# Converting w_out two feature blocks at a time, and two small sums as fp32r products, in a fused attention / soft-MoE / feed-forward kernel

## The chip, the cores and the metric

One core of one Trainium2 chip runs the whole program. The metric is device microseconds of one execution, from the start of the program to the last output in memory. The kernel before takes 477.78 us, the median of three executions (477.72 to 479.6).

## What is computed

Three stages run one after the other; the change lies in the third.

```python
x = _attn_ref(q, k, v, mem_k, mem_v)          # chunked attention, 4 x 768 tokens, 8 heads of 64
x = _moe_ref(x, phi, w1, w2)                  # soft mixture: c @ slot_out, c is 3072 x 32, slot_out 32 x 512
h = x @ w_in                                  # w_in 512 x 2048
r = np.maximum(h, 0.0)
g = s * (r * r) + b
out = g @ w_out                               # w_out 2048 x 512, out 3072 x 512
```

Since x = c @ slot_out, the kernel forms m = slot_out @ w_in (32 x 2048) once and h = c @ m. The constant b goes through w_out as b times its column sums, which are added to the output at the end, so the products only see r * r.

## The kernel before

**Two 16-bit halves.** TensorE multiplies fp32r operands at one rate and plain f32 operands as two instructions of a slower one. The large products are done in fp32r, and each operand is split into a high part (a cast to fp32r) and a low part (value minus high part): `ghi`/`glo` for r * r, `w_hi`/`w_lo` for w_out. Three products of a pair (high x high, low x high, high x low) make one output. w_in and w_out come in as 16-bit halves of their words, and every block has to be put together on ScalarE and VectorE before it is split.

**One block of w_out, 128 rows x 512.** `stage_a(k)` is a ScalarE copy with a scale (`cv_act`, line 579). `stage_d(k, 0..5)` are six VectorE instructions: a shift (589), an or with the sign (591), a mask (593), the low half times the exponent (600), value minus `w_hi` (791), plus the low half (793), which writes `w_lo`. `stage_w(k)` is the cast to `w_hi` on ScalarE (798). The table `cq` says at which step k a block is converted: w_out blocks 0 to 7 at steps 0, 2, .. 14, four quarters each of w_in's column groups 2 and 3 at steps 16 to 30, w_out blocks 8 to 15 at steps 32 to 46. Two buffers `cvs` alternate.

**The item loop.** `items` holds 128 pairs (run, f): a run is 384 tokens and a stretch of w_out's 16 blocks. The first 16 items are blocks 0 to 7 of token groups 0 and 1 in turn, the next 32 all blocks of groups 2 and 3 in turn, then groups 4 to 7 alone, then blocks 8 to 15 of groups 0 and 1. Step n emits `emit_h(n)` (line 825, one product of 384 columns into a PSUM tile of the tag "s", which has two buffers), the nine products of 512 columns of older items (`emit_o`, line 877, of item n-3, six of them; `emit_o2`, line 889, of item n-4, three), `emit_relu`, `emit_sq`, `emit_ghi` (ScalarE, 831, 835, 839: relu out of PSUM, square, cast) and `emit_g` (VectorE, 842: the low part of item n-1). When a run ends, its three PSUM tiles are copied out (894 and 896), and the next run on the same tiles waits for that. Steps 0 to 3 are written out by hand ahead of the loop: the ramp.

**Order.** The schedule is manual: each engine runs its instructions in the order in which the program emits them.

**m.** Column group 0 of m (blocks 0 to 3 of w_in's 2048 columns) is done in the ramp by `m_part` and `m_split`. Group fb = 1, 2, 3 comes at step n of `M_AT = (4, 26, 34)`: `emit_m` (806) puts four partial sums on four groups of 32 partitions of a PSUM tile of tag "s", a ScalarE copy (808) brings them to `mps`, and at step n+1 `emit_m2` (812) adds them with a 0/1 matrix `stks_all` in a plain f32 product of 512 columns, into another tile of tag "s"; `m_split` (817 on ScalarE, 818 on VectorE) writes the high and the low part into `mpack`, the stationary operand of line 825. In each step `emit_m` and `emit_m2` stand behind `emit_relu`, `emit_sq` and `emit_ghi`.

**Column sums.** From step 48 to 63 `wsum_add` adds `w_hi` and `w_lo` of all blocks on VectorE, and at step 64 `colsum` (852) sums over partitions by an f32 product with ones; line 853 scales it into `bias`.

**Loads.** `load_w` issues one weight load on the sync engine's queue, in a fixed order. Behind the first ones the loads go round a ring of three areas, each issued as soon as the last use of the block it overwrites (`last_use`) has been emitted.

Of the kernel before, what the change touches and what calls it, by code (L numbers as in the profile page):

```python
# [8 lines left out]
F32 = mybir.dt.float32  # L9
F32R = mybir.dt.float32r  # L10
I32 = mybir.dt.int32
# [24 lines left out]
def kernel(  # L36
# [81 lines left out]
    with tc.manual_schedule():  # L118
# [60 lines left out]
        raw_of = {("i", fb, j): ("wi", 2 * fb + j // 2) for fb in range(1, NFB) for j in range(4)}  # L179
        raw_of.update({("o", f): ("wo", f // 2) for f in range(NF)})  # L180
        last_use = {}
        for k, key in sorted(cq.items()):
            if raw_of[key] not in last_use:
                order.append(raw_of[key])
            last_use[raw_of[key]] = k
# [5 lines left out]
        def load_w(n, cap=None):  # L191
            for _ in range(n):
                i = wnext[0]
                if i < (len(order) if cap is None else cap):
                    src = srcs[order[i][0]][order[i][1]]
                    p = at_[order[i]] if i < npre else (16 + (i - npre) % NRG) * SLOT
# [369 lines left out]
        soT4 = area(15 * SLOT + 1536, KD, 4, NS)  # L566
        sos_r = Ring(14 * SLOT + 1536, 2, 256)
# [150 lines left out]
        for i in range(16):  # L718
            emit_w2(i)
            if i == 4:  # L720
                left.close()
                pk_p = ctx.enter_context(tc.tile_pool(name="pk", bufs=1, reuse_waits="tile"))
                cpack = pk_p.tile([128, NT], F32R, name="cpack")
                mpack = pk_p.tile([128, 128 * NF], F32R, name="mpack")
            if i in (3, 7, 11):
# [28 lines left out]
        w_hi, w_lo = tiles("whi", NF, DM, F32R), tiles("wlo", NF, DM, F32R)  # L754
        os_g, mps = tiles("os", 3, DM), tiles("mps", 1, DM)[0]
        r_g, r2_g = (tiles(x, 2, UT) for x in ("r", "r2"))
        ghi_g, glo_g = tiles("ghi", LA + 2, UT, F32R), tiles("glo", LA + 2, UT, F32R)
        wsum, bias = tiles("wsum", 1, DM)[0], tiles("bias", 1, DM)[0]
        ones = tiles("ones", 1, 128)[0]
        nc.gpsimd.memset(ones, 1.0)  # L760
# [11 lines left out]

        def stage_a(k):
            key = cq.get(k)
            if key:
                if key[0] == "i":
                    w = wi_src(key[1], key[2])
                else:
                    w = wt[raw_of[key]].rearrange("p (f d t) -> p f d t", f=2, t=2)[:, key[1] % 2]
# [20 lines left out]
        def emit_m(fb):  # L800
# [129 lines left out]
        stage_a(0)  # L930
# [3 lines left out]
        stages(0, 0)  # L934
# [5 lines left out]
        stages(0, 1)  # L940
# [23 lines left out]
        stage_a(4)  # L964
        stages(2, 2, 3)
        emit_g(3)
        stages(2, 4, 5)
        stages(4, 0)
        for n in range(LA + 1, len(items) + LA + 1):
# [29 lines left out]
            stage_d(n + 1, 0)  # L999
            if 48 <= n < 64:  # L1000
# [80 lines left out]
```

## Time and profile before

| | |
|---|---|
| median of 3 executions | 477.78 us (477.72 to 479.6) |
| the profiled execution, whole | 481.1 us |
| its span, first to last instruction | 479.3 us |
| TensorE matmul busy | 455.8 us (95%), 3960 instructions |
| VectorE busy | 309.6 us (65%) |
| ScalarE busy | 307.6 us (64%) |
| GpSimd busy | 84.1 us (18%) |
| mean granted TensorE clock | 0.999 of 2.4 GHz |

The 1.8 us between 479.3 and 481.1 lie around the span. Busy shares are means over stages: attention until about 124 us, the expert products (bound by the loads of their weights) until about 171 us, the ramp of the last stage until about 190 us, and then the item loop until 474 us. A busy TensorE says little by itself, since matmuls overlap and a waiting one can be counted as busy. What ends the execution is read from the chain of waits, and what a step costs from the starts of line 825, which comes once in each step.

### The profile page before, as it was taken

The page shows a single profiled execution, that of the slowest core. Times are in us where ns is not written, and L with a number is a line of the kernel's source. Part 1 is how long each engine was busy: PE and PEld are TensorE (multiplying, and loading weights), DVE is VectorE, ACT ScalarE, POOL GpSimd, SP SyncE. Part 2 cuts the span into 40 slices and gives each one's busy share as a digit, 9 for nine tenths or more (in the row PEclk, how much of TensorE's full clock was granted, in tenths as well). Part 3 has the DMA queues.
Part 4 walks back from the last instruction along what each step waited for, and adds up shares of the span by engine and source line. Part 5 has one row for each costly group of instructions (what it writes and reads, how often), then busy time and mean ns, then how long its engine had stood idle before and what let it go on. Part 6 is the DMA issues. An engine that isn't in the chain of part 4 may idle for free.

```text
span 479.3 us, 10204 instructions
## 1 busy us (share of the span) xinstructions
PE 455.8 (95%) x3960; PEld 342.8 (72%) x3960; DVE 309.6 (65%) x685; ACT 307.6 (64%) x635; POOL 84.1 (18%) x154
## 2 busy tenths in 40 slices
PE   6889998999999878999999999999999999999996
PEld 5656666665545365886787888887888888888885
DVE  5768888886485867999485999985624224223232
ACT  4556665665134357998686888666666666666660
POOL 6665655560000000000000000006700000000000
PEclk9999999999999999999999999999999999999999
DMA  8999999999999932333332000003101001001011
GB/s 302 371 406 403 399 408 401 392 384 402 384 408 383 416 137 88 116 150 96 115 142 88 1 1 0 1 0 131 69 0 67 0 1 66 0 1 65 2 66 66
DMA packets 20576, 83.04 MB, mean 173 GB/s; under 512 B 2736, under 2 KB 2864, under 8 KB 14640
## 3 DMA queue, kind: packets, MB, share of 16 engines
q1 hardware_dynamic: 20528, 82.39, 44.5%
q8 instruction: 31, 0.51, 0.4%
q14 instruction: 17, 0.14, 0.1%
HBM read 76.09 MB, written 6.29 MB: 172 GB/s over the span
## 4 chain that ended last, share of the span: by engine, by line
PE 68%; DVE 12%; DMA 10%; ACT 4%; issue 2%; POOL 2%; SPq 1%; DVEq 0%; POOLq 0%; ACTq 0%
PE g L877 11%; PE lp L877 5%; PE pt L877 5%; PE x L877 5%; PE g L889 5%; PE xt L877 5%; PE s L825 4%; DMA keys<-in_w_out_dram 4%; DMA vals<-in_vm_dram 3%; PE s L630 3%; PE x L325 3%; PE lp L889 3%; PE pt L889 3%; PE xt L889 3%; PE x L889 3%; PE s L285 2%
## 5 line engine op out<-in xcount | busy, mean ns | idle before, releaser
L842 DVE TENSOR_TENSOR glo<-r,ghi 128x384 fp32r<-128x384 f32 x128 | 76.3, 600 | 81.4 <-ACT ghi L839 81.2
L831 ACT ACTIVATE r<-s 128x384 f32<-128x384 f32 x128 | 62.7, 490 | 52.7 <-PE s L825 52.4
L835 ACT ACTIVATE r<-r 128x384 f32<-128x384 f32 x128 | 67.2, 525 | 9.7 <-DVE glo L842 5.6
L839 ACT CAST ghi<-r 128x384 fp32r<-128x384 f32 x128 | 65.4, 511 | 3.4
L825 PE MATMUL s<-cpack,mpack 128*128 128x384 f32 x128 | 44.7, 352 | 1.9 <-DVE mpack L818 1.9
L301 ACT ACTIVATE seg<-seg 128x384 f32<-128x384 f32 x32 | 28.7, 897 | 19.2 <-DVE seg L312 15.3
L889 PE MATMUL g<-wlo,ghi 128*128 128x512 f32 x128 | 40.2, 394 | 0.0
L877 PE MATMUL g<-whi,ghi 128*128 128x512 f32 x126 | 39.7, 394 | 0.3 <-DVE mpack L818 0.3
L877 PE MATMUL g<-whi,glo 128*128 128x512 f32 x126 | 39.4, 393 | 0.0
L864 POOL TENSOR_TENSOR keys<-keys,bias 128x512 f32<-128x512 f32 x6 | 8.4, 1430 | 169.4 <-DVE bias L853 169.4
L263 POOL TENSOR_SCALAR keys<-keys 64x416 f32<-64x416 f32 x63 | 33.6, 533 | 14.2 <-DMA keys<-in_kq_dram 7.4
L285 PE MATMUL s<-keys 128*32 128x128 f32 x768 | 30.3, 291 | 5.0 <-POOL keys L267 4.2
L325 PE MATMUL x<-vals,seg 128*32 128x128 f32 x744 | 28.0, 275 | 3.6 <-DMA vals<-in_vm_dram 2.9
L825 PEld LDWEIGHTS s<-cpack,mpack 128*128 128x128 f32 x128 | 23.9, 188 | 9.5 <-DVE mpack L818 2.0
L325 PEld LDWEIGHTS x<-vals,seg 128*32 128x32 f32 x744 | 20.5, 109 | 13.3 <-DVE seg L309 4.6
L889 PEld LDWEIGHTS g<-wlo,ghi 128*128 128x128 f32 x128 | 24.0, 188 | 5.2
L877 PEld LDWEIGHTS g<-whi,glo 128*128 128x128 f32 x126 | 23.7, 188 | 5.4
L285 PEld LDWEIGHTS s<-keys 128*32 128x32 f32 x768 | 19.5, 113 | 11.0 <-POOL keys L267 6.5
L319 ACT COPY seg<-pt 128x384 f32<-128x384 f32 x32 | 15.2, 476 | 18.5 <-PE pt L317 17.6
L877 PEld LDWEIGHTS g<-whi,ghi 128*128 128x128 f32 x126 | 23.7, 188 | 4.4 <-DVE mpack L818 0.7
L877 PE MATMUL lp<-whi,ghi 128*128 128x512 f32 x63 | 25.5, 404 | 0.9 <-DVE vals L896 0.9
L877 PE MATMUL pt<-whi,glo 128*128 128x512 f32 x64 | 25.3, 395 | 0.7 <-DVE glo L842 0.7
(255 smaller groups left out, 990.6 us busy)
## 6 DMA issues: line engine op xcount, KB each, us to landing
seg<-in_w_dram SPq DMA_DIRECT2D x27, 1024.0 KB, 8.5
keys<-in_kq_dram SPq DMA_DIRECT2D x32, 396.0 KB, 7.3
vals<-in_vm_dram SPq DMA_DIRECT2D x64, 192.0 KB, 6.6
keys<-in_w_in_dram SPq DMA_DIRECT2D x5, 1024.0 KB, 5.1
keys<-in_w_out_dram SPq DMA_DIRECT2D x5, 1024.0 KB, 4.9
out_dram<-os SPq DMA_DIRECT2D x18, 256.0 KB, 2.1
vals<-in_w_in_dram SPq DMA_DIRECT2D x3, 1024.0 KB, 7.7
vals<-in_w_out_dram SPq DMA_DIRECT2D x3, 1024.0 KB, 4.8
```

What stands on the lines that cost most here:

```text
L263: (nc.vector if h and u == 0 else nc.gpsimd).tensor_scalar(out=stream(kz[rows, h], 0, CH), in0=k[rows, UT * h:UT * h + (NCU + 1) * CH].rea ...
L285: nc.tensor.matmul(out=o, lhsT=qt[:, 32 * c:32 * c + 32], rhs=kz[:, :, at:at + WIN], start=True, stop=not (first or last))
L301: nc.scalar.activation(out=p_r[u], in_=sm_r[u].rearrange("p t h (a r) -> p t r (h a)", a=2), func=AF.Exp, scale=scale)
L319: nc.scalar.copy(out=pts_r[u], in_=pt)
L325: nc.tensor.matmul(out=xp[32 * r:32 * r + 32, t], lhsT=pts_r[u][:, 32 * c:32 * c + 32], rhs=vbuf[u // 2 % 2][:, u % 2, :, 64 * c:64 * c + ...
L825: nc.tensor.matmul(out=hq, lhsT=mpack[:, 128 * f:128 * f + 128], rhs=cpack[:, b * UT:(b + 1) * UT], start=True, stop=True)
L831: nc.scalar.activation(out=r_g[n % 2], in_=h_t.pop(n), func=AF.Relu)
L835: nc.scalar.activation(out=r2_g[n % 2], in_=r_g[n % 2], func=AF.Square)
L839: nc.scalar.copy(out=ghi_g[n % (LA + 2)], in_=r2_g[n % 2])
L842: nc.vector.tensor_tensor(out=glo_g[n % (LA + 2)], in0=r2_g[n % 2], in1=ghi_g[n % (LA + 2)].bitcast(F32), op=ALU.subtract)
L877: nc.tensor.matmul(out=o_t[r_][t], lhsT=gt[:, 128 * t:128 * t + 128], rhs=w_hi[f], start=(f == r_[1] and gt is ghi), stop=False)
L889: nc.tensor.matmul(out=o, lhsT=ghi[:, 128 * t:128 * t + 128], rhs=w_lo[f], start=False, stop=(f == f1 - 1))
```

## The change

It touches only the last stage and its preparations.

- Blocks 0 and 1 of w_out are converted as before at steps 0 and 2. Blocks 2 to 15 are converted in seven pairs (`pair_a`, `pair_d` 0 to 3, `pair_hi`) with instructions of 2 x 512 columns, the pair i beginning at step `PS[i]` (4, 7, 10, 31, 34, 38, 42); `pair_a` comes one step earlier, `pair_hi` one step later.
- `stage_a(0)` moves behind the first `m_split`, and the first VectorE steps of block 0 behind the second.
- `mps` is split in two: `mph` (ScalarE cast) and `mpl` (VectorE, value minus `mph`), and `emit_m2` becomes two fp32r products that accumulate. `colsum` does the same with `wsum`.
- In the item loop, `emit_m` and `emit_m2` move ahead of `emit_relu`, `emit_sq`, `stage_a` and `emit_ghi` of their step.
- Two constants, the 0/1 matrix and ones, are cast to fp32r on ScalarE during the expert products; the GpSimd memset of `ones` goes.
- `bias` shares its memory with `wsum`. The ring of loads lies in other areas, `soT4` and `sos_r` move, and the second of the first three ring loads is issued one product group later (the loop over 16 products: at 10, 11 and 14 in place of 10, 10 and 14).

```diff
         for j in range(8):
+            cq[16 + 2 * j] = ("i", 2 + j // 4, j % 4)
+        for j in range(2):
             cq[2 * j] = ("o", j)
-            cq[16 + 2 * j] = ("i", 2 + j // 4, j % 4)
-            cq[32 + 2 * j] = ("o", 8 + j)
...
+        PS = {1: 4, 2: 7, 3: 10, 4: 31, 5: 34, 6: 38, 7: 42}
+        last_use = {("wi", 4 + j // 2): 16 + 2 * j for j in range(8)}
+        last_use.update({("wo", i): n + 1 for i, n in PS.items()})
+        last_use["wo", 0] = 2
+        RAW = [17 * SLOT, 18 * SLOT, 14 * SLOT]
...
+                nc.scalar.copy(out=stkr, in_=stks_all)
+                nc.scalar.activation(out=onesr, in_=stks_all, func=AF.Copy, scale=0.0, bias=1.0)
...
-            if i == 10:
-                load_w(2)
-            if i == 14:
+            if i in (10, 11, 14):
                 load_w(1)
...
+        def pair_a(i):
+            nc.scalar.activation(out=pair[:, :, 0, :], in_=pair_w(i)[:, :, :, 1].bitcast(F32), func=AF.Copy,
+                                 scale=2.0 ** -112)
+        def pair_hi(i):
+            nc.scalar.copy(out=two(wh_all, i), in_=pair[:, :, 2, :])
+        def pair_d(i, step):
+            h, lf, a = (pair[:, :, j, :] for j in range(3))
+            hi, ai, w = h.bitcast(I32), a.bitcast(I32), pair_w(i)
+            if step == 0:
+                nc.vector.tensor_scalar(out=hi, in0=hi, scalar1=3, scalar2=None, op0=ALU.logical_shift_left)
+                nc.vector.scalar_tensor_tensor(out=ai, in0=w[:, :, :, 1], scalar=SIGN, in1=hi, op0=ALU.bitwise_and,
+                                               op1=ALU.bitwise_or)
+            elif step == 1:
+                nc.vector.tensor_scalar(out=hi, in0=ai, scalar1=EXPM, scalar2=None, op0=ALU.bitwise_and)
+                nc.vector.scalar_tensor_tensor(out=lf, in0=w[:, :, :, 0].bitcast(U32), scalar=2.0 ** -52, in1=h,
+                                               op0=ALU.mult, op1=ALU.mult)
+            elif step == 2:
+                nc.vector.tensor_tensor(out=a, in0=a, in1=two(wh_all, i).bitcast(F32), op=ALU.subtract)
+            else:
+                nc.vector.tensor_tensor(out=two(wl_all, i), in0=a, in1=lf, op=ALU.add)
...
-            nc.scalar.copy(out=mps, in_=mp)
+            halves(mp)
+
+        def halves(x):
+            nc.scalar.copy(out=mph, in_=x)
+            nc.vector.tensor_tensor(out=mpl, in0=x, in1=mph.bitcast(F32), op=ALU.subtract)
+
+        def sum_of(out, lhsT):
+            for x in (mph, mpl):
+                nc.tensor.matmul(out=out, lhsT=lhsT, rhs=x, start=(x is mph), stop=(x is mpl))
...
-            nc.tensor.matmul(out=mr, lhsT=stks_all, rhs=mps, start=True, stop=True)
+            sum_of(mr, stkr)
...
-            nc.tensor.matmul(out=c, lhsT=ones, rhs=wsum, start=True, stop=True)
+            halves(wsum)
+            sum_of(c, onesr)
...
-        stage_a(0)
         m_part(mpa, (2, 3), ha)
         m_split(mpa, 0, ha)
         m_part(mpb, (2, 3), hb)
-        stages(0, 0)
+        stage_a(0)
         m_split(mpb, 0, hb)
...
-        stage_a(4)
         stages(2, 2, 3)
+        pair_a(1)
         emit_g(3)
         stages(2, 4, 5)
-        stages(4, 0)
...
+            if n in M_AT:
+                emit_m(M_AT.index(n) + 1)
+            if n - 1 in M_AT:
+                emit_m2(M_AT.index(n - 1) + 1)
             emit_relu(n)
             emit_sq(n)
             stage_a(n + 1)
             emit_ghi(n)
-            if n in M_AT:
-                emit_m(M_AT.index(n) + 1)
-            if n - 1 in M_AT:
-                emit_m2(M_AT.index(n - 1) + 1)
...
+            for i, p0 in PS.items():
+                if n == p0 + 1:
+                    pair_hi(i)
+                if 0 <= n - p0 < 4:
+                    pair_d(i, n - p0)
+                if n == p0 - 1:
+                    pair_a(i)
```

## Rows read from the trace of the kernel before

**Rows 1.** Windows: each engine's busy us (instructions), clock, DMA share, GB/s
```profile
151.70:171.00 19.30, 16.06 (x186) 8.75 (x182) 12.08 (x22) 6.81 (x17) 0.20 (x1) 1.00 1.01 416
...
215.00:220.00 5.00, 4.14 (x17) 2.60 (x16) 4.90 (x9) 4.71 (x10) 0.00 (x0) 1.00 0.02 2
...
260.00:300.00 40.00, 40.00 (x179) 33.01 (x178) 38.63 (x70) 33.29 (x68) 0.00 (x0) 1.00 0.00 1
```

**Rows 2.** Timeline of PE, line 825, at the first runs' end: start us, us, instruction
```profile
212.82 0.34 PE L825 MATMUL s<-cpack,mpack 128*128 128x384 f32 x1
...
215.08 0.34 PE L825 MATMUL s<-cpack,mpack 128*128 128x384 f32 x1
...
217.79 0.34 PE L825 MATMUL s<-cpack,mpack 128*128 128x384 f32 x1
...
221.36 0.34 PE L825 MATMUL s<-cpack,mpack 128*128 128x384 f32 x1
```

**Rows 3.** Timeline of the ramp's head, in brackets the idle time before and its releaser
```profile
170.74 0.66 ACT L579 ACTIVATE seg<-keys 128x512 f32<-128x512 f32 x1 [2.38 <-DMA keys<-in_w_out_dram]
171.31 0.25 ACT L817 CAST mpack<-pt 128x128 fp32r<-128x128 f32 x1
...
171.94 0.62 PE L825 MATMUL s<-cpack,mpack 128*128 128x384 f32 x2 [1.85 <-DVE mpack L818]
...
174.30 0.39 PE L877 MATMUL pt<-whi,ghi 128*128 128x512 f32 x1
```

**Rows 4.** Timeline of PE later in the ramp: the two longest waits
```profile
183.72 1.13 PE L812 MATMUL s<-mps,stk 128*128 128x512 f32 x2 [0.82 <-ACT mps L808]
...
188.50 0.50 PE L877 MATMUL pt<-whi,glo 128*128 128x512 f32 x1 [0.70 <-DVE glo L842]
```

**Rows 5.** Chain of waits, 196 to 205 us: start us, us, engine, tile, line
```profile
198.61 0.42 DVE keys L589
199.03 0.47 DVE glo L842
...
203.00 0.42 DVE seg L589
```

**Rows 6.** Timeline of DVE in the same stretch: start us, us, instruction
```profile
202.39 0.69 DVE L793 TENSOR_TENSOR wlo<-keys 128x512 fp32r<-128x512 f32 x1
...
203.34 0.55 DVE L842 TENSOR_TENSOR glo<-r,ghi 128x384 fp32r<-128x384 f32 x1
```

**Rows 7.** Instructions of line 817 by form: duration ns min/median/max, first and last start
```profile
L817 ACT CAST mpack<-s x3: 583/586/586, 186.6 to 259.9; 128x512 fp32r<-128x512 f32 x3
...
L817 ACT CAST mpack<-g x1: 366/366/366, 175.4 to 175.4; 128x256 fp32r<-128x256 f32 x1
```

**Rows 8.** Groups by line and form, 195 to 480 us: busy us, mean ns, idle before
```profile
L579 ACT ACTIVATE keys<-keys 128x512 f32<-128x512 f32 x6 | 4.0, 659 | 0.0
```

**Rows 9.** Chain of waits around the second group of m: start us, us
```profile
235.05 1.21 PE s L806 x12
236.26 0.37 PE s L825
...
238.70 0.86 PE s L812 x2
239.96 0.47 PE g L877 x2
```

**Rows 10.** Chain of waits at step 64
```profile
325.37 0.86 PE s L852 x2
```

**Rows 11.** Waits, 166 to 222 us: us in total, times, longest
```profile
PEld s L806 <- ACT r L831: 0.4, 1, 0.4
```

**Rows 12.** Timeline of ACT in steps 26 and 27, idle time before in brackets
```profile
233.01 0.49 ACT L831 ACTIVATE r<-s 128x384 f32<-128x384 f32 x1 [0.25 <-PE s L825]
...
236.31 0.59 ACT L808 COPY mps<-s 128x512 f32<-128x512 f32 x1 [1.70 <-PE s L806]
236.79 0.50 ACT L831 ACTIVATE r<-s 128x384 f32<-128x384 f32 x1
```

More of the change, by code (lines that the diff above doesn't have):

```diff
@@ L175 @@
         for j in range(8):
+            cq[16 + 2 * j] = ("i", 2 + j // 4, j % 4)
+        for j in range(2):
             cq[2 * j] = ("o", j)
-            cq[16 + 2 * j] = ("i", 2 + j // 4, j % 4)
-            cq[32 + 2 * j] = ("o", 8 + j)
[L179 to L185, printed above, removed]
+        PS = {1: 4, 2: 7, 3: 10, 4: 31, 5: 34, 6: 38, 7: 42}
+        last_use = {("wi", 4 + j // 2): 16 + 2 * j for j in range(8)}
+        last_use.update({("wo", i): n + 1 for i, n in PS.items()})
+        last_use["wo", 0] = 2
+        order += [("wo", i) for i in range(4)] + [("wi", i) for i in range(4, 8)] + [("wo", i) for i in range(4, 8)]
+        RAW = [17 * SLOT, 18 * SLOT, 14 * SLOT]
         srcs = {"w1": w1, "w2": w2, "wi": w_in, "wo": w_out}
@@ L195, in load_w @@
                     src = srcs[order[i][0]][order[i][1]]
-                    p = at_[order[i]] if i < npre else (16 + (i - npre) % NRG) * SLOT
+                    p = at_[order[i]] if i < npre else RAW[(i - npre) % NRG]
                     if p is SPLIT:
@@ L565 @@
         cvs = [area((14 + i) * SLOT, 3, 512) for i in range(2)]
-        soT4 = area(15 * SLOT + 1536, KD, 4, NS)
-        sos_r = Ring(14 * SLOT + 1536, 2, 256)
+        soT4 = area(16 * SLOT + 1024, KD, 4, NS)
+        sos_r = Ring(16 * SLOT + 1536, 2, 256)
         ck_r = [area(p, 4, 4, NS).bitcast(F32R) for p in range(11 * SLOT, 11 * SLOT + NT, 512)]
@@ L724 @@
                 mpack = pk_p.tile([128, 128 * NF], F32R, name="mpack")
+                stkr = pk_p.tile([128, 128], F32R, name="stkr")
+                onesr = pk_p.tile([128, 128], F32R, name="onesr")
+                nc.scalar.copy(out=stkr, in_=stks_all)
+                nc.scalar.activation(out=onesr, in_=stks_all, func=AF.Copy, scale=0.0, bias=1.0)
             if i in (3, 7, 11):
@@ L752, in tiles @@
             return [g_p.tile([128, w], dt, name=f"{name}{i}") for i in range(n)]
-        w_hi, w_lo = tiles("whi", NF, DM, F32R), tiles("wlo", NF, DM, F32R)
-        os_g, mps = tiles("os", 3, DM), tiles("mps", 1, DM)[0]
+        wh_all, wl_all = (tiles(x, 1, NF * DM, F32R)[0] for x in ("whi", "wlo"))
+        w_hi, w_lo = ([t[:, DM * f:DM * f + DM] for f in range(NF)] for t in (wh_all, wl_all))
+        os_g, (mph, mpl) = tiles("os", 3, DM), tiles("mp", 2, DM, F32R)
         r_g, r2_g = (tiles(x, 2, UT) for x in ("r", "r2"))
         ghi_g, glo_g = tiles("ghi", LA + 2, UT, F32R), tiles("glo", LA + 2, UT, F32R)
-        wsum, bias = tiles("wsum", 1, DM)[0], tiles("bias", 1, DM)[0]
-        ones = tiles("ones", 1, 128)[0]
-        nc.gpsimd.memset(ones, 1.0)
+        wsum = tiles("wsum", 1, DM)[0]
+        bias = wsum
         HF = NF // 2
@@ L771, with pair_w, two @@
         h_t, o_t = {}, {}
+        cvs[:] = [area(15 * SLOT + 1536 * x, 3, 512) for x in range(2)]
+        pair = area(15 * SLOT, 3072).rearrange("p (x j f) -> p x j f", x=2, j=3)
+        def pair_w(i):
+            return wt["wo", i].rearrange("p (f d t) -> p f d t", f=2, t=2)
+        def pair_a(i):
[3 more added lines that the diff above has]
+            nc.scalar.copy(out=two(wh_all, i), in_=pair[:, :, 2, :])
+        def two(t, i):
+            return t[:, 2 * DM * i:2 * DM * (i + 1)].rearrange("p (x f) -> p x f", x=2)
+        def pair_d(i, step):
[13 more added lines that the diff above has]
+                nc.vector.tensor_tensor(out=two(wl_all, i), in0=a, in1=lf, op=ALU.add)
         def stage_a(k):
@@ L778, in stage_a @@
                 else:
-                    w = wt[raw_of[key]].rearrange("p (f d t) -> p f d t", f=2, t=2)[:, key[1] % 2]
+                    w = wt["wo", key[1] // 2].rearrange("p (f d t) -> p f d t", f=2, t=2)[:, key[1] % 2]
                 cv_act(key, k // 2 % 2, w)
@@ L939 @@
         m_part(mpc, range(KD), hc)
-        stages(0, 1)
+        stages(0, 0, 1)
         nc.vector.tensor_copy(out=w_hi[0], in_=cv[cq[0]][2])
```

## The prediction, made before the changed kernel ran

> **What bounds the kernel now.** I read the windows first, then the starts of line 825, then the chain of waits, and the timelines of ScalarE and VectorE only where the chain leaves TensorE. The windows [rows 1] show three regimes: up to 171 us the queues move 416 GB/s and the weights set the pace; from 215 to 220 us VectorE is busy for 4.90 of 5 us while TensorE has a hole (4.14); from 260 to 300 us TensorE is busy throughout, though VectorE nearly is as well (38.63 of 40). The starts of line 825 tell what each step costs: 2.26 us when nothing waits (212.82 to 215.08), but 2.71 and 3.57 us for the two steps at the end of the first runs, 0.45 + 1.31 = 1.76 us too much [rows 2]. From 221.36 us to the last product at about 474 us the chain of waits stays on TensorE. So what TensorE loses or saves there moves the end one for one, and work taken from ScalarE and VectorE there is worth nothing. Before 221 us there are four places to gain: 1.85 us ahead of h(0) [rows 3], 0.82 us ahead of the sum of m's group 1 and 0.70 us ahead of item 4's low product [rows 4], and the 1.76 us.
>
> **The head of the ramp.** ScalarE waits 2.38 us for the first block of w_out, and the first copy of m stands behind that conversion; h(0) starts at 171.94 us [rows 3]. Turned round, h(0) leaves the path. Late next is `w_hi[0]`: the conversion still starts at 170.74 and takes until 171.3, the second copy of m and its VectorE part stand ahead of the shift (about 0.6 us together), and shift, or and cast take some 1.6 us, so about 173.5 us. Item 0's first product ran at 174.30 [rows 3]: -0.8 us.
>
> **Pairs.** Converting one block costs VectorE 203.00 - 198.61 = 4.39 us less two low parts of 0.47, so 3.45 us in six instructions [rows 5]. From 384 to 512 columns an instruction grows from 0.55 to 0.69 us [rows 6], 1.1 ns a column; that leaves about 0.1 us an instruction that does not grow, 0.6 us for six. A pair thus takes 6.3 us instead of 6.9 (an estimate from these rows; 6.9 if nothing is saved). VectorE before needs 4.39 us for two steps of 4.52: no reserve. After, three pairs save 1.8 us and the last ends at step 13 rather than 15, so VectorE is ahead when the first runs end, and the 1.76 us of [rows 2] go: -1.76. If a backlog is left, some or all of that comes back. At ScalarE an instruction grows by 0.86 ns a column (586 against 366 ns for 256 more [rows 7]); the conversion becomes 1.10 us instead of twice 0.66 [rows 8], the cast about the same, some 0.4 us less per pair, which nobody on the path feels.
> But a pair is ready later: item 4 needs `w_hi[2]` after a shift, an or and a cast that are each up to twice as long, some 1.2 us more in all, and `w_lo` follows likewise. I put the waits for the two at 1.0 and 0.6 us where 0.70 us stood [rows 4], and 0.1 us more at item 1: +1.0. Bounds: -0.7 if the pair is early, +2 if both wait an instruction longer. The later pairs begin three or four steps ahead of use, and their loads are issued eight or more steps ahead: nothing, as long as VectorE, which with 6.3 + 3 x 0.47 = 7.7 us needs 0.9 us more than three steps of 2.26, makes that up in the steps without a pair.
>
> **The two-part sums.** An f32 sum of 512 columns took 0.86 us, two fp32r products take 2 x 0.235 = 0.47 [rows 9], so -0.4 us at each of four places. In the ramp (step 4) the copy no longer stands behind relu, square and cast; but `pair_a(1)`, 1.1 us long, now does stand ahead of it, the low part (about 0.7 us on VectorE) must be there as well, and relu(4) behind the copy holds h(5). I take these as equal to the 0.82 us of before [rows 4], so -0.4 net, with 0.8 us to either side. At step 64 the copy of `wsum` starts when ScalarE is through with the step's cast, and the low part follows, 0.6 + 0.7 us, of which the products of the step cover about half; the second product waits some 0.5 us, so that the step costs 0.1 to 0.4 us more than with the 0.86 us [rows 10]; I take +0.2. The bias, which replaces `wsum` in place, waits for nothing new.
>
> **Copies ahead of relu, steps 26, 27, 34 and 35.** Here is the cost. Tag "s" has two buffers. In order they go to h(26), m's partial sums, h(27), the sum, h(28): h(27) needs the one that relu(26) reads, h(28) the one that relu(27) reads. That such a wait is real shows in the ramp, where line 806 waits 0.4 us for relu [rows 11]. Before, relu(26) ran at 233.01 us, while TensorE did the step's products, and the copy waited until 236.31 with nothing urgent behind it [rows 12]. Now relu(26), its square and its cast queue behind the copy: copy at 236.31, relu at 236.79, over at 237.29, and only then h(27), which ran at 236.26 [rows 9]. That is 1.05 us, of which 0.1 to 0.2 us was lost there already (0.37 us for a product of 0.18). The same a step later: from the end of the sum 0.03 + 0.48 us until relu, 0.50 us of relu, then h(28): again 1.0 to 1.2 us, less the 0.40 us that the sum saves. One group: +1.6 us by these rows, +2.0 if the array gives its results as late behind the shorter products (a lone product lasts 0.39 us [rows 3] in a slot of 0.235, 0.16 us twice). Two groups: +3.2 to +4.0, I take +3.6. On VectorE's queue glo(25) and the conversions wait behind the low part and behind `m_split`'s; they have slack, since item n's low part is read at step n+3.
> The row shows ScalarE holding back a copy whose input was ready, for a load that the copy did not need [rows 3]. The Trainium skill (TensorE: Matmul & The Clock Gate, Architectural detail) says that ScalarE and VectorE are strictly first in, first out, and that TensorE alone pulls weight loads ahead. By that rule, with which the trace agrees, the sum keeps its +3.6 us; an engine that let relu pass would give the time of the first rival.
>
> **Moved and small.** The two casts of constants (128 columns, about 0.25 us each) and the new areas of the ring lie in the expert products, where loads at 416 GB/s set the pace [rows 1]; the ring's second load, issued later on the sync engine's queue, still stands behind several us of queued bytes. If that cover were gone, it would come a few us later, but it is needed some 8 us after the first. GpSimd's memset held nobody on the path.
>
> **Sum.** -0.8 - 1.76 + 1.0 - 0.4 + 3.6 + 0.2 = +1.8 us. The profiled execution took 481.1 us in all, so 482.9 on its own terms. It is 3.3 us longer than the median; were some of that the first block of w_out landing later than it usually does, h(0) would usually not wait for it and up to 0.8 us of gain would be lost. On the median: 477.8 + 1.8 = 479.6 us. Its own range, by the bounds above, is 477.8 to 481.6.
>
> **Rivals.**
> *Faster: relu does not hold TensorE.* If h(27) and h(28) found a free buffer, the two groups would give 2 x -0.4 instead of +3.6: 479.6 - 4.4 = 475.2. For it: the sums are 0.4 us cheaper each. Against it: [rows 11], and all eight PSUM tiles (two "s", two "g", "pt", "x", "xt", "lp") being in use.
> *Slower: the pair's strided parts wait for each other as one area.* The parts of `pair` interleave in memory; if waits are set for the whole range, the mask waits for the cast to `w_hi` (about 1.1 us) and the next pair's conversion for the subtraction. VectorE's 7.7 us for three steps become 8.8 against 6.78, 2.0 us late at each of the three gaps of three steps; of these 6.0 us some 1.5 are caught up: +4.5, so 484.1. It decides as soon as a pair's chain passes three steps and the reserve behind it. Against it: nothing before has such a wait.
> *The run's end stays.* If VectorE is still late at step 18, the 1.76 us remain: 481.4.
>
> **How the numbers follow.** Forecast 0.62, faster rival 0.14, waits within the pair 0.12, run's end 0.12. About 0.5%, 2.4 us, is what a measurement of this kernel can tell from no change: 475.4 to 480.2. Three fifths of the forecast lie inside it, the rest above; of the faster rival two thirds lie below. So faster 0.10, same 0.43, slower 0.47. Range: the forecast's own and the run's end, stretched down to the faster rival: 475.0 to 482.0, which leaves out the waits within the pair and the tails.
>
> **What would show it.** Line 825 of steps 27, 28, 35 and 36 should start about 1 us late behind a wait for line 831, with relu right behind the copy on ScalarE; the two products of a sum should stand 0.23 us apart; the steps at the first runs' end should take 2.26 us with no wait for an evacuation; item 0's first product should come about 0.8 us earlier; and there should be a short TensorE wait for the low part ahead of the column sums. I am wrong if TensorE waits for nothing at those four steps, or if a pair's instructions wait for each other across engines.

## The result, and the profile after

The changed kernel takes 481.8 us, the median of nine executions (480.64 to 484.09), beside 478.74 us for the kernel before on the same chip (nine executions, 477.72 to 480.36). The ratio is 1.0073, with a 95% interval of 1.005 to 1.0095: slower by 2.4 to 4.5 us. The forecast was +1.8 us. Its sign and its main mechanism hold, but the size is short by about half.

The waits of TensorE in the last stage of the kernel after, in us in total, times and longest (line 873 is relu, 867 h, 920 and 932 the products of the items, 786 the pair's cast to `w_hi`, 805 its `w_lo`, 846 the low part of a sum, 850 the sum):

```profile
PE s L867 <- ACT r L873: 4.6, 5, 1.1
PE pt L920 <- ACT whi L786: 0.9, 1, 0.9
PE s L850 <- DVE mp L846: 0.5, 2, 0.3
PE pt L932 <- DVE wlo L805: 0.5, 1, 0.5
```

The first line is the one the prediction asked for: h waits for relu, about 1.07 us at each of four steps and once, for 0.35 us, in the ramp. No wait for an evacuation is left. The starts of h at the first runs' end, where [rows 2] had 2.71 and 3.57 us, are 2.26 us apart:

```profile
211.43 0.34 PE L867 MATMUL s<-cpack,mpack 128*128 128x384 f32 x1
213.69 0.34 PE L867 MATMUL s<-cpack,mpack 128*128 128x384 f32 x1
215.95 0.34 PE L867 MATMUL s<-cpack,mpack 128*128 128x384 f32 x1
218.20 0.34 PE L867 MATMUL s<-cpack,mpack 128*128 128x384 f32 x1
```

Two windows answer to [rows 1] (busy us and instructions of TensorE, weight loads, VectorE, ScalarE, GpSimd; clock, DMA share, GB/s):

```profile
213.00:218.00 5.00, 5.00 (x24) 4.12 (x23) 4.93 (x10) 4.76 (x10) 0.00 (x0) 1.00 0.23 39
264.00:304.00 40.00, 40.00 (x179) 33.04 (x178) 33.51 (x48) 32.25 (x61) 0.00 (x0) 1.00 0.00 1
```

At the run ends TensorE has no hole any more. VectorE is as busy as before in this one window, but over the whole steps from h(18) to h(21) it has less to do. Here are these steps in the kernel before, then in the kernel after (the third group of numbers is VectorE):

```profile
212.82:221.36 8.54, 7.68 (x31) 5.29 (x30) 8.37 (x16) 7.38 (x16) 0.00 (x0) 1.00 0.32 107
```
```profile
211.43:218.20 6.77, 6.77 (x31) 5.59 (x30) 6.28 (x12) 5.79 (x13) 0.00 (x0) 1.00 0.20 44
```

VectorE has 12 instructions in place of 16. In the later stretch VectorE is 5 us lighter (33.51 against 38.63), and the items take as long as ever.

Steps 26 to 28 of the kernel after, the answer to [rows 9] and [rows 12], on TensorE, then ScalarE, then VectorE:

```profile
229.50 0.34 PE L867 MATMUL s<-cpack,mpack 128*128 128x384 f32 x1
...
231.85 1.06 PE L840 MATMUL s<-seg,keys 128*32 128x512 f32 x8
...
234.20 0.44 PE L867 MATMUL s<-cpack,mpack 128*128 128x384 f32 x1 [1.07 <-ACT r L873]
...
236.54 0.63 PE L850 MATMUL s<-mp,stkr 128*128 128x512 f32 x2
238.24 0.44 PE L867 MATMUL s<-cpack,mpack 128*128 128x384 f32 x1 [1.07 <-ACT r L873]
...
240.61 0.33 PE L867 MATMUL s<-cpack,mpack 128*128 128x384 f32 x1
```
```profile
233.17 0.59 ACT L845 CAST mp<-s 128x512 fp32r<-128x512 f32 x1 [3.54 <-PE s L840]
233.65 0.50 ACT L873 ACTIVATE r<-s 128x384 f32<-128x384 f32 x1
...
237.21 0.59 ACT L859 CAST mpack<-s 128x512 fp32r<-128x512 f32 x1 [1.96 <-PE s L850]
237.69 0.50 ACT L873 ACTIVATE r<-s 128x384 f32<-128x384 f32 x1
```
```profile
233.79 0.69 DVE L846 TENSOR_TENSOR mp<-s,mp 128x512 fp32r<-128x512 f32 x1 [4.11 <-ACT mp L845]
```

h(26) starts at 229.50 us, so its relu could have run before 230 us. ScalarE stands idle for 3.54 us in front of the copy of m's partial sums, and relu comes only behind that, at 233.65 us. h(27) follows at once. The same happens at 237.69 and 238.24 us. The Trainium skill (TensorE: Matmul & The Clock Gate, Architectural detail) says that ScalarE takes its queue strictly first in, first out; the 3.54 us in front of a ready relu agree.

**A measure that does not move.** The spread between executions (over 3 us) is as large as the effect. Most of it lies ahead of the last stage: the last expert product starts at 164.33 to 166.70 us in these profiles. So I measured each profile from the start of the last expert product (line 668) to the starts of h. A second execution of the kernel before and two kernels that turned out to be worth the same (e3_before_loads, e9_before_head) give 298.00, 297.98 and 297.97 us to h(127). Where the first block of w_out lands as there, the measure repeats to hundredths, and a tenth of a microsecond can be read. The table splits this distance at h(12), h(25), h(62) and h(67): the ramp, the first runs' end, the two groups of m at steps 26 to 36, and the column sums. Steps of 2.26 us without a wait would be 29.38, 83.62 and 11.30 us for the second to fourth column.

| kernel | ramp, to h(12) | to h(25) | to h(62) | to h(67) | line 668 to h(127) |
|---|---|---|---|---|---|
| before, the profile read for the prediction | 32.56 | 31.12 | 88.06 | 12.13 | 299.47 |
| before, run again (e0_before) | 31.07 | 31.13 | 88.06 | 12.14 | 298.00 |
| after | 31.55 | 29.37 | 92.26 | 12.63 | 301.41 |
| e1_relu_first | 31.53 | 29.37 | 87.96 | 12.64 | 297.10 |
| e2_before_sums_early | 29.20 | 31.12 | 92.28 | 12.14 | 300.34 |
| e3_before_loads | 31.06 | 31.13 | 88.06 | 12.13 | 297.98 |
| e4_f32_sums | 30.84 | 29.37 | 88.06 | 12.12 | 295.99 |
| e5_no_pairs | 30.02 | 30.92 | 92.24 | 12.63 | 301.41 |
| e7_before_ramp_early | 29.19 | 31.13 | 88.06 | 12.13 | 296.11 |
| e8_mixed | 30.62 | 29.46 | 88.06 | 12.12 | 295.86 |
| e9_before_head | 31.05 | 31.12 | 88.06 | 12.14 | 297.97 |
| e10_one_pair | 29.18 | 31.43 | 88.06 | 12.12 | 296.39 |
| e11_colsum_apart | 29.20 | 31.44 | 88.06 | 11.74 | 296.04 |
| e12_mixed_colsum | 30.61 | 29.45 | 88.06 | 11.75 | 295.47 |

After against e0_before: 0.48 - 1.76 + 4.20 + 0.49 = +3.41 us, which is what the timed ratio gives (0.0073 x 478.7 = 3.5). Against the profile read for the prediction it would be only +1.94, because that execution had a slow ramp of its own, 1.5 us longer.

### The profile page after: what moved, and what is told of

The parts are those of the page before. It is cut to its first block, busy times and chain, and to the rows that moved or that the text cites. A ratio compares the mean times of both kernels' runs of the same rounds, so it can differ in the third digit from the quotient of the medians.

```text
span 480.9 us, 10167 instructions
## 1 busy us (share of the span) xinstructions
PE 454.3 (94%) x3960; PEld 342.0 (71%) x3960; DVE 308.0 (64%) x647; ACT 309.6 (64%) x624; POOL 84.2 (18%) x153
## 4 chain that ended last, share of the span: by engine, by line
PE 73%; DVE 9%; DMA 8%; ACT 4%; issue 2%; SPq 2%; POOL 1%; DVEq 0%; POOLq 0%; ACTq 0%
PE g L920 12%; PE g L932 6%; PE pt L920 6%; PE lp L920 6%; PE x L920 6%; PE xt L920 6%; DMA seg<-in_w_dram 5%; PE s L867 5%; PE s L630 3%; PE pt L932 3%; PE lp L932 3%; PE xt L932 3%; PE x L932 3%; PE x L325 3%; PE s L285 2%
## 5 line engine op out<-in xcount | busy, mean ns | idle before, releaser
L867 PE MATMUL s<-cpack,mpack 128*128 128x384 f32 x128 | 43.7, 344 | 4.9 <-ACT r L873 4.6
L907 POOL TENSOR_TENSOR keys<-keys,wsum 128x512 f32<-128x512 f32 x6 | 8.4, 1423 | 200.4 <-ACT r L873 200.4
L920 PE MATMUL pt<-whi,ghi 128*128 128x512 f32 x64 | 25.7, 401 | 0.9 <-ACT whi L786 0.9
L932 PE MATMUL pt<-wlo,ghi 128*128 128x512 f32 x64 | 25.5, 398 | 0.7 <-DVE wlo L805 0.5
```

What stands on the lines that cost most here:

```text
L867: nc.tensor.matmul(out=hq, lhsT=mpack[:, 128 * f:128 * f + 128], rhs=cpack[:, b * UT:(b + 1) * UT], start=True, stop=True)
L920: nc.tensor.matmul(out=o_t[r_][t], lhsT=gt[:, 128 * t:128 * t + 128], rhs=w_hi[f], start=(f == r_[1] and gt is ghi), stop=False)
L932: nc.tensor.matmul(out=o, lhsT=ghi[:, 128 * t:128 * t + 128], rhs=w_lo[f], start=False, stop=(f == f1 - 1))
```

## The experiments

All ratios are to the kernel before, whose executions ran in turn on the same chip. "The eleventh step" of the expectations is h(12), the eleventh row of h: two rows hold two products each.

**e0_before: the kernel before once more,** with no edit.

> The kernel before, unchanged, for a second profile of its ramp. In the first profile the first block of w_out landed at 170.66 us, 4.0 us behind the start of the last expert product, and held h(0); in the changed kernel's profile the conversion ran without a wait at 169.45, 3.1 us behind that product. Theory A (the late landing belonged to that one execution): here the conversion waits less for its load, and from the last expert product's start to h(12) it takes 31.0 to 31.8 us instead of 32.56. Theory B (the landing is late in every execution because the second block is issued together with the first): again about 32.5 us, and ScalarE waits some 2.4 us for the load.

It took 477.77 us, and 31.07 us from the last expert product to h(12): theory A. ScalarE, then TensorE, at the head of its ramp:

```profile
167.37 0.67 ACT L579 ACTIVATE seg<-keys 128x512 f32<-128x512 f32 x1 [0.86 <-DMA keys<-in_w_out_dram]
```
```profile
164.85 0.64 PE L668 MATMUL xt<-seg,seg 128*32 128x256 f32 x8 [0.35 <-DMA seg<-in_w_dram]
...
168.58 0.61 PE L825 MATMUL s<-cpack,mpack 128*128 128x384 f32 x2 [0.35 <-DVE mpack L818]
...
170.93 0.39 PE L877 MATMUL pt<-whi,ghi 128*128 128x512 f32 x1
```

The wait for the first block of w_out is 0.86 us, not the 2.38 of [rows 3], and h(0) waits 0.35 us, not 1.85. Item 0's first product comes 170.93 - 164.85 = 6.08 us after the last expert product.

**e3_before_loads: the second ring load issued later,** nothing else.

```diff
-            if i == 10:
-                load_w(2)
-            if i == 14:
+            if i in (10, 11, 14):
                 load_w(1)
```

> The kernel before with one part of the change: the ring's second load is issued one product group later (10, 11, 14 in place of 10, 10, 14). Theory B: the first block lands about 1 us earlier, h(0) no longer waits for it, and the time falls by 0.8 to 1.6 us. Theory A: no change beyond 0.3 us.

478.33 us, ratio 0.9988 (0.997 to 1.0007), and the table's row is that of e0_before to 0.02 us. The load's new place costs and gives nothing; its wait for the block is again 0.88 us. The late block belonged to one execution.

**e1_relu_first: relu back ahead of the sums,** everything else as after.

```diff
+            emit_relu(n)
             if n in M_AT:
                 emit_m(M_AT.index(n) + 1)
             if n - 1 in M_AT:
                 emit_m2(M_AT.index(n - 1) + 1)
-            emit_relu(n)
             emit_sq(n)
```

> The changed kernel with one line moved: in each step relu comes first again, then the copies and sums of m, then square and cast. Theory (relu behind the copies holds h(27), h(28), h(35), h(36)): the four waits for line 873 of 1.07 us each vanish, the time falls by 4.0 us against the changed kernel, which brings it 0.5 to 1 us below the kernel before. Rival (the four waits only use up slack that is lost elsewhere, for instance in the loads or in VectorE's conversions): it stays within 1 us of the changed kernel, 2.5 us or more above the kernel before.

477.26 us, ratio 0.9982 (0.9963 to 1.0002). The waits of TensorE:

```profile
PE s L850 <- DVE mp L846: 1.0, 2, 0.8
PE pt L932 <- DVE wlo L805: 1.0, 1, 1.0
PE s L867 <- DVE mpack L860: 0.7, 2, 0.5
```

No wait for relu is left. One moved line takes 4.30 us off the two groups (92.26 to 87.96) and leaves the ramp as it was (31.55 and 31.53). The whole slowdown is this order.

**e2_before_sums_early: the kernel before with only that order,** the sums ahead of relu at all three places.

```diff
-            emit_relu(n)
-            emit_sq(n)
-            stage_a(n + 1)
-            emit_ghi(n)
             if n in M_AT:
                 emit_m(M_AT.index(n) + 1)
             if n - 1 in M_AT:
                 emit_m2(M_AT.index(n - 1) + 1)
+            emit_relu(n)
+            emit_sq(n)
+            stage_a(n + 1)
+            emit_ghi(n)
```

> The kernel before with only the move: emit_m and emit_m2 ahead of relu in each step; sums stay f32, conversions stay single. Theory: the same waits at steps 27, 28, 35 and 36, about 1.07 us each and 4.2 to 4.8 us together, less 1 to 1.5 us that the earlier copy gives in the ramp: +2.8 to +3.5 us against the kernel before. Rival (the waits come from the two-part sums or the pairs, not from the order): no such waits and a time within 0.5 us of before or faster.

480.59 us, ratio 1.0047 (1.0028 to 1.0066). The groups cost 4.22 us more, as in the kernel after, although the sums here are plain f32. And the ramp is 1.87 us shorter. TensorE, then ScalarE, in steps 26 and 27:

```profile
232.54 0.45 PE L825 MATMUL s<-cpack,mpack 128*128 128x384 f32 x1 [0.68 <-ACT mps L808]
...
234.91 1.02 PE L812 MATMUL s<-mps,stk 128*128 128x512 f32 x2
237.00 0.44 PE L825 MATMUL s<-cpack,mpack 128*128 128x384 f32 x1 [1.07 <-ACT r L831]
```
```profile
231.91 0.58 ACT L808 COPY mps<-s 128x512 f32<-128x512 f32 x1 [3.55 <-PE s L806]
232.39 0.50 ACT L831 ACTIVATE r<-s 128x384 f32<-128x384 f32 x1
```

Here h(27) starts at 232.54 us while relu(26), begun at 232.39, is still running. So it does not take relu's buffer, but the one that the copy of the partial sums has just given back. In the kernel after, VectorE reads the partial sums as well, from 233.79 us on and for 0.69 us. h(27) starts at 234.20 us, before VectorE is through, so there it takes the buffer of relu(26) and waits for it. The two kernels differ in which buffer the program gives h(27).

**e4_f32_sums: e1_relu_first, and both kinds of sums plain f32 again.**

```diff
-            halves(mp)
+            nc.scalar.copy(out=mps, in_=mp)
...
-            sum_of(mr, stkr)
+            nc.tensor.matmul(out=mr, lhsT=stks_all, rhs=mps, start=True, stop=True)
...
-            halves(wsum)
-            sum_of(c, onesr)
+            nc.tensor.matmul(out=c, lhsT=onesr, rhs=wsum, start=True, stop=True)
```

> The kernel after with relu back ahead of the sums (as in the run with relu first, 477.3 us, ratio 0.998) and, further, both kinds of sums as plain f32 products again: m's partial sums are copied once and added in one f32 product, and the column sums likewise; the pairs stay. Theory A (the two-part form costs as much as it saves, because its second product waits for the low part on VectorE, which the trace of the kernel after shows as 0.2 to 0.3 us a sum, and 0.8 us with relu first): the step of the column sums falls from 5.85 to about 5.35 us, the two groups give -0.1 to -0.4 us in all, the ramp stays within 0.3 us: about 476.6 us, ratio 0.996. Theory B (the prediction's term, 0.4 us saved by each two-part sum): -0.2 us at the column sums, +0.8 us in the two groups, +0.4 us in the ramp: about 478.3 us, ratio 1.000.

475.97 us, ratio 0.9948 (0.993 to 0.9966): theory A for the whole, but not for each part. The two-part form cost 0.52 us at the column sums (12.64 to 12.12), as theory A had it, and 0.69 us in the ramp (31.53 to 30.84), twice what it allowed. In the two groups together it had gained 0.10 us, against theory A: about 0.4 us in the first group, of which about 0.3 us were lost in the second. There h(37) waits for VectorE, which reads the sum for its low part late, behind two instructions of a pair; TensorE, then VectorE, in e1_relu_first:

```profile
257.74 0.44 PE L867 MATMUL s<-cpack,mpack 128*128 128x384 f32 x1 [0.47 <-DVE mpack L860]
```
```profile
256.99 0.69 DVE L860 TENSOR_TENSOR mpack<-s,mpack 64x512 fp32r<-64x512 f32 x1
```

**e5_no_pairs: the kernel after with every block of w_out converted alone.**

```diff
+            cq[2 * j] = ("o", j)
             cq[16 + 2 * j] = ("i", 2 + j // 4, j % 4)
-        for j in range(2):
-            cq[2 * j] = ("o", j)
+            cq[32 + 2 * j] = ("o", 8 + j)
...
-        PS = {1: 4, 2: 7, 3: 10, 4: 31, 5: 34, 6: 38, 7: 42}
+        PS = {}
...
+        stage_a(4)
         stages(2, 2, 3)
-        pair_a(1)
         emit_g(3)
         stages(2, 4, 5)
+        stages(4, 0)
```

> The kernel after without the pairs: every block of w_out is converted by itself at the steps of the kernel before; the order of the sums, their two-part form and the head of the ramp stay as after. Both theories have the first runs' end wait again (2.7 and 3.6 us for the two steps in place of 2.26, +1.76 us). Theory A (the prediction's price, the pairs cost 1.0 us in the ramp): +0.8 us against the kernel after, ratio to before about 1.009. Theory B (the pairs cost the ramp over 2 us, and the sums ahead of relu hid that, as the kernel before with the sums ahead of relu has a ramp 1.9 us shorter): from the last expert product to the eleventh step 29.2 us as there in place of 31.5, so -0.5 us against the kernel after, ratio to before about 1.006.

481.7 us, ratio 1.0068 (1.005 to 1.0086), and 301.41 us to h(127), to the hundredth what the kernel after has. The pairs give 1.55 us at the first runs' end (30.92 to 29.37) and take 1.53 us in the ramp (30.02 to 31.55). This lies between the two theories. The rest of what theory B expected in the ramp is the sum itself; TensorE and VectorE at step 5:

```profile
181.28 0.73 PE L853 MATMUL s<-mp,stkr 128*128 128x512 f32 x2 [1.11 <-DVE mp L849]
```
```profile
180.54 0.69 DVE L849 TENSOR_TENSOR mp<-s,mp 128x512 fp32r<-128x512 f32 x1
```

TensorE stands 1.11 us for the low part, which VectorE makes only when its conversions let it. Between e2_before_sums_early (f32 sums, 29.20) and this run (30.02) the ramp differs by 0.82 us. They also differ in the head and the loads, both of which alone moved nothing (e9_before_head, e3_before_loads), so the 0.82 us is the two-part form.

**e7_before_ramp_early: the kernel before with the sums early in the ramp alone,** and right behind relu in the later groups.

```diff
+            if n > LA + 2:
+                emit_relu(n)
+            if n in M_AT:
+                emit_m(M_AT.index(n) + 1)
+            if n - 1 in M_AT:
+                emit_m2(M_AT.index(n - 1) + 1)
+            if n <= LA + 2:
+                emit_relu(n)
-            emit_relu(n)
             emit_sq(n)
             stage_a(n + 1)
             emit_ghi(n)
-            if n in M_AT:
-                emit_m(M_AT.index(n) + 1)
-            if n - 1 in M_AT:
-                emit_m2(M_AT.index(n - 1) + 1)
```

> The kernel before with the sums ahead of relu in the ramp alone (group 1, steps 4 and 5), and right behind relu, ahead of the square and the cast, in the two later groups; nothing else changes. Theory A (where relu does not have to free a buffer at once, the sums ahead of it are a gain): ramp -1.9 us, the two groups -0.3 to -0.8 us in all, run ends unchanged: about 475.9 us, ratio 0.995. Theory B (what the ramp gains is lost again at the first runs' end, as VectorE is late there): the steps of 2.71 and 3.57 us grow by what the ramp gave, 477.7 us, ratio 0.998 to 1.000.

476.0 us, ratio 0.9954 (0.9939 to 0.997). The ramp's 1.88 us reach the end; the run ends are as before, so theory B falls. The groups stay at 88.06: their place right behind relu gave none of the 0.3 to 0.8 us that theory A hoped for.

**e8_mixed: single blocks where they are needed at once, pairs behind them.** The order of e7_before_ramp_early, the f32 sums of e4_f32_sums, and

```diff
-        for j in range(2):
+        for j in range(4):
             cq[2 * j] = ("o", j)
...
-        PS = {1: 4, 2: 7, 3: 10, 4: 31, 5: 34, 6: 38, 7: 42}
+        PS = {2: 8, 3: 11, 4: 31, 5: 34, 6: 38, 7: 42}
```

> The kernel after with four edits: blocks 2 and 3 of w_out converted one by one and only blocks 4 to 15 in pairs (the first two pairs at steps 8 and 11); the sums ahead of relu in the ramp alone and right behind relu later; both kinds of sums as plain f32 products. Theory A (only the first pair costs the ramp, since its blocks are needed at once, and the later pairs give VectorE the reserve that ends the waits at the first runs' end): ramp -1.9 us, run ends -1.8 us, the two groups -0.3 to -0.8 us against the kernel before: about 474.2 us, ratio 0.991. Theory B (VectorE is the bound over the whole of steps 4 to 18, so that pairs from step 8 on come too late for the run ends): about 1.8 us more, 476.0 us, ratio 0.995.

475.16 us, ratio 0.9933 (0.9915 to 0.9951). The run ends are free of waits, but the ramp pays again at the first pair:

```profile
192.98 0.50 PE L920 MATMUL pt<-whi,ghi 128*128 128x512 f32 x1 [0.86 <-ACT whi L787]
```

So theory A holds for the run ends and not for the ramp. In the profile the kernel is 0.25 us ahead of e7_before_ramp_early (295.86 against 296.11). The timed gain over before, 3.2 us (2.3 to 4.1), is larger than the 2.1 us seen behind the last expert product; what else it holds, I did not find.

**e10_one_pair: only blocks 6 and 7 as a pair in the ramp,** otherwise e8_mixed.

```diff
-        PS = {2: 8, 3: 11, 4: 31, 5: 34, 6: 38, 7: 42}
+        PS = {3: 12, 4: 31, 5: 34, 6: 38, 7: 42}
```

> The kernel of the run with blocks 2 and 3 single, once more with fewer pairs in the ramp: blocks 2 to 5 single and only blocks 6 and 7 as a pair, from step 12 on; sums plain f32, ahead of relu in the ramp alone. That run showed 1.1 us of waiting for the high parts of its first pair. Theory A (a pair saves VectorE 0.9 us, and the waits at the first runs' end shrink by that, while its high parts are ready in time): ramp as without pairs (29.2 us from the last expert product to the eleventh step), run ends 0.9 us in place of 1.76: 474.5 us, ratio 0.992. Theory B (a pair costs its 1.1 us of waiting wherever VectorE has no reserve): no better than two pairs, 475.2 us, ratio 0.993 or above.

476.86 us, ratio 0.9978 (0.996 to 0.9997): theory B. The waits for the pair are the same, only later:

```profile
PE pt L919 <- ACT whi L786: 0.9, 1, 0.9
PE pt L931 <- DVE wlo L805: 0.7, 1, 0.7
```

The pair does free the run ends of their waits, more than theory A asked. But its own two waits come ahead of them, and with them this stretch takes 31.43 us, 2.05 more than steps without a wait, where single blocks take 1.75 more (e7_before_ramp_early).

**e9_before_head: the kernel before with the new head alone.**

```diff
-        stage_a(0)
         m_part(mpa, (2, 3), ha)
         m_split(mpa, 0, ha)
         m_part(mpb, (2, 3), hb)
-        stages(0, 0)
+        stage_a(0)
         m_split(mpb, 0, hb)
...
-        stages(0, 1)
+        stages(0, 0, 1)
```

> The kernel before with the head of the ramp alone in the order of after: the first block's ScalarE conversion behind the first copy of m, its first VectorE step behind the second low part of m. Theory A (the 0.8 us of the prediction belonged to one execution in which the first block of w_out landed late; where ScalarE waits 0.9 us for it, not 2.4, h(0) waits for nothing that the order could save): h(0) comes 0.1 us earlier after the last expert product (3.62 in place of 3.73 us), the fourth step at the same time, the whole within 0.2 us: ratio 1.000. Theory B (the order is worth its 0.8 us): item 0's first product 0.8 us earlier, 477.6 us, ratio 0.998.

478.44 us, ratio 0.9996 (0.9979 to 1.0013), 297.97 us to h(127): theory A, the new head is worth nothing when the block lands as it usually does.

**e11_colsum_apart and e12_mixed_colsum: the column sums in two parts, a step after their split.** The edit, on top of e10_one_pair and of e8_mixed (left out here: the column sums are two fp32r products again, the copy of m's partial sums goes into `wsum`, and `add_bias` comes a step later):

```diff
             if n == 64:
+                halves(wsum)
+            if n == 65:
                 colsum()
```

> As the run with one pair in the ramp, and the column sums as two fp32r products again, with the split into halves at step 64 and the two products a step later, at step 65 (so the additions of the bias come a step later too). Theory A (the two-part form pays where a step lies between the split and the products): steps 62 to 67 take about 11.8 us in place of 12.13, so 0.35 us less than the run with one pair. Theory B (the gain of a shorter small product never reaches the end): no difference of 0.1 us or more in these steps.

> The run with blocks 2 and 3 single and the other blocks in pairs (475.2 us, ratio 0.993), with the one edit of the column sums added: split at step 64, the two products at step 65. If the gains add, steps 62 to 67 take 11.75 us in place of 12.12, and the whole is 0.4 us shorter: 474.8 us, ratio 0.9925. If the ramp's two waits for the first pair differ from execution to execution, the sum is lost in their spread, and only the steps 62 to 67 show it.

476.19 us, ratio 0.9956 (0.9937 to 0.9975), and 475.55 us, ratio 0.9946 (0.9927 to 0.9965). Both times steps 62 to 67 take 0.37 to 0.38 us less (11.74 and 11.75 in place of 12.12): theory A. Now the low part is long done when TensorE comes to the two products, here in e11_colsum_apart, first VectorE, then TensorE:

```profile
320.66 0.69 DVE L846 TENSOR_TENSOR mp<-wsum,mp 128x512 fp32r<-128x512 f32 x1 [2.22 <-ACT mp L845]
```
```profile
322.66 0.64 PE L850 MATMUL s<-mp,onesr 128*128 128x512 f32 x2
323.13 0.34 PE L867 MATMUL s<-cpack,mpack 128*128 128x384 f32 x1
```

e12_mixed_colsum has the shortest last stage of all, 295.47 us, 2.53 less than the kernel before. By the timed ratios e8_mixed, e12_mixed_colsum and e4_f32_sums can't be told apart; all are faster than the kernels before and after.

## Why the prediction was right or wrong

**Copies ahead of relu: right, +4.20 us where +3.6 stood,** just above the bounds of 3.2 to 4.0. The wait, its place, its cause and its four steps were as forecast, and e1_relu_first takes all of it back. What was mis-sized is the 0.40 us that each shorter sum was to give back. It is there (from the start of the sum to h(28) it is 1.70 us after, 2.09 in e2_before_sums_early), but the step ahead loses the same: 4.70 us from h(26) to h(27) against 232.54 - 228.24 = 4.30. With plain f32 sums h(27) takes the buffer of the partial sums and waits for the copy alone; with the two-part form it takes relu's and waits for relu. It is the form that does this and not the pairs, for e5_no_pairs, with the two-part form and single blocks, has the same 4.70 us:

```profile
233.23 0.44 PE L870 MATMUL s<-cpack,mpack 128*128 128x384 f32 x1 [1.07 <-ACT r L876]
```

The prediction knew that h(27) waits for relu(26), but took it as given by the order of the buffers; with f32 sums it would not. In the prediction's own two steps, against e0_before: +1.14 us where 0.85 to 0.95 stood, as nothing of the wait was "lost there already", and +0.95 us where 0.6 to 0.8 stood.

**The head: wrong, 0 where -0.8 stood.** This is the step that failed most: the prediction's sum took the wait of 2.38 us for the first block of w_out as one that every execution has. The row was right, but for one execution; in the next the wait was 0.86 us (e0_before), and the new head alone gave nothing (e9_before_head). That the profile was 3.3 us above the median was the warning, and the prediction named the doubt and what it would cost; it still kept the gain in the sum. In the kernel after, ScalarE does not wait for the block, and the first product comes at the same distance as in e0_before:

```profile
169.45 0.67 ACT L579 ACTIVATE keys<-keys 128x512 f32<-128x512 f32 x1
```
```profile
166.32 0.64 PE L668 MATMUL xt<-seg,seg 128*32 128x256 f32 x8 [0.38 <-DMA seg<-in_w_dram]
...
172.40 0.47 PE L920 MATMUL pt<-whi,ghi 128*128 128x512 f32 x1
```

172.40 - 166.32 = 6.08 us.

**Run ends: right, -1.76 us,** for the reason given, a lighter VectorE; of it the pairs alone give 1.55 us (e5_no_pairs). A pair was put at 6.3 us for its six instructions. It takes 6.0:

```profile
190.17 0.69 DVE L795 TENSOR_SCALAR keys<-keys 128x1024 int32<-128x1024 int32 x1
190.90 1.22 DVE L796 SCALAR_TENSOR_TENSOR keys<-seg,keys 128x1024 int32<-128x1024 int32 x1
192.04 0.55 DVE L884 TENSOR_TENSOR glo<-r,ghi 128x384 fp32r<-128x384 f32 x1
192.51 0.69 DVE L799 TENSOR_SCALAR keys<-keys 128x1024 int32<-128x1024 int32 x1
193.23 1.22 DVE L800 SCALAR_TENSOR_TENSOR keys<-seg,keys 128x1024 f32<-128x1024 uint32 x1
194.37 0.55 DVE L884 TENSOR_TENSOR glo<-r,ghi 128x384 fp32r<-128x384 f32 x1
194.84 1.22 DVE L803 TENSOR_TENSOR keys<-keys,whi 128x1024 f32<-128x1024 f32 x1
```

From start to start the first five are 0.73, 1.14, 0.72, 1.14 and 1.14 us, the sixth the same again: 6.01.

**Pairs in the ramp: +1.53 us where +1.0 stood** (the kernel after against e5_no_pairs), within the bounds of -0.7 to +2. The two waits are there, 0.88 and 0.46 us beside the forecast 1.0 and 0.6, but the two steps that hold them, to h(7) and to h(9), are 1.13 and 0.73 us longer than in e5_no_pairs. Two more steps change: the one to h(5) is 0.43 us longer, with a wait of 0.35 us for relu(4), and the one to h(6) is 0.81 us shorter, as TensorE waits 0.28 us for the low part of the sum and not 1.11. That the pairs' loss in the ramp would eat up their whole gain at the run ends (e5_no_pairs) the prediction did not see.

**The sum in the ramp: -1.05 us where -0.4 stood, and for other reasons.** The order was taken as neutral and the form as a gain of 0.4. The order alone gives -1.87 us (e2_before_sums_early): both waits of [rows 4] are gone, since the ramp waits for m and not for relu. The form costs +0.82. The gains do not add freely either: with pairs and two-part sums in place, the order moves the ramp by 0.02 us (after against e1_relu_first). There the waits only change places: for relu, the low part, `w_hi` and `w_lo` they are 0, 0.78, 0.34 and 0.97 us in e1_relu_first, and 0.35, 0.28, 0.88 and 0.46 in the kernel after. So the split into +1.53 and -1.05 holds only when the pairs are taken last. e4_f32_sums, with pairs and with f32 sums right behind relu, has a ramp 0.23 us shorter than e0_before.

**Column sums: +0.49 us where +0.2 stood,** above the bounds of 0.1 to 0.4. The wait for the low part was named, but the first product was thought to be covered by the step; it too came late, behind ScalarE's cast, which ended at 326.51 us. TensorE, in the kernel after:

```profile
326.57 0.50 PE L850 MATMUL s<-mp,onesr 128*128 128x512 f32 x1
327.29 0.50 PE L850 MATMUL s<-mp,onesr 128*128 128x512 f32 x1 [0.23 <-DVE mp L846]
327.63 0.34 PE L867 MATMUL s<-cpack,mpack 128*128 128x384 f32 x1
```

**The sum of the misses:** 0.8 (head) + 0.5 (pairs) - 0.65 (sum in the ramp) + 0.6 (groups) + 0.3 (column sums) = 1.55 us, and 1.8 + 1.55 = 3.35, what the table shows (3.41) but for rounding. Five terms were off. The two of the ramp nearly cancel (+0.6 stood for pairs and sum together, +0.48 was measured), and that is luck, since neither was right. What is left is the head, the groups and the column sums, which all pointed one way.

**The rivals.** Relu did hold TensorE. The pair's strided parts did not wait for each other: the mask of the first pair started at 184.97 us, while the cast to `w_hi` ran from 184.71 for 1.04 us, and in all seven pairs the mask started before the cast was over. The wait at the end of the runs did not stay.

**Left open.** What the pairs cost in the ramp of the kernel before, with f32 sums in the old order, which no run has; why the first block of w_out landed late in one execution; and what the 1.1 us of timed gain of e8_mixed are that its last stage does not show.

## What to carry to other kernels

Ask of every instruction put ahead of another on an in-order engine whether its own input is there yet. If it is not, everything behind it waits as well, and a buffer behind that may stop the engine that mattered. The same move can be a gain at one place (the ramp, -1.9 us with f32 sums and single blocks, nothing with pairs and two-part sums) and a loss at another (+2.1 us a group), so move it only where it gains. Splitting an operand to make a small product cheaper can pay when a step lies between the split and the product (-0.38 us at the column sums), and costs when the product waits for the second half (+0.5 to +0.8 us). Before a stall of one profile goes into a sum, see it in a second execution.

## What the runs showed of the hardware that was not expected

A second reader costs a PSUM buffer its early release. The partial sums were free 0.05 us after the copy's end when ScalarE alone read them (e2_before_sums_early: copy until 232.49, h(27) at 232.54). The sum that VectorE reads behind ScalarE was free only when VectorE was done (e1_relu_first: line 860 until 257.68, h(37) at 257.74).

Doubling a VectorE instruction of 512 columns took 0.42 us to 0.69 for the forms with one source tensor and 0.69 us to 1.22 for those with two. A block cost 3.45 us, a pair 6.01, so some 0.15 us an instruction does not grow, not the 0.1 of the prediction's estimate. The Trainium skill (VectorE: DVE Perf Modes, The TRN2 errata) gives (N + 151) cycles at 0.96 GHz for an f32 add of two tensors: 691 ns for 512 columns, and as an estimate from it 1224 ns for 1024. The trace agrees, with 0.69 us for line 793 before and 1.22 us for the subtraction of line 803 after.
